# Attention stage of an attention and two-MoE kernel: another order of first loads, first products, weight splits and last slot sums

## The chip, the cores and the metric

The kernel runs on one core of a Trainium2 chip. The metric is the device time of one execution in microseconds (us); smaller is better. The engines are TensorE (PE), VectorE (DVE), ScalarE (ACT), GpSimd (POOL) and SyncE (SP); SP, ACT and POOL also issue the transfers (DMA).

## The reference

Attention with a decaying state, then two mixtures of experts (MoE), each sending a token to one of eight experts:

```python
for t in range(S):                       # 2 batches, 8 heads, S = 768, D = 64
    state = gamma * state + einsum('bhd,bhe->bhde', k[:, :, t], v[:, :, t])
    y[:, :, t] = scale * einsum('bhd,bhde->bhe', q[:, :, t], state)
x = y as 1536 tokens of 512
# first MoE: only tokens with x @ w_skip > 0; expert = argmax of x @ w_gate, gate = its softmax
out = x;  out[those] = x + gate * (relu(x @ w1[e]) @ w2[e])
# second MoE: all tokens, up to `capacity` for each expert; the others give 0
out = gate * (relu(x @ w1[e]) @ w2[e])
```

## The kernel before

**Tiling.** The 768 positions are six chunks `c` of 128, and each chunk has two units `(c, b)`, one for each batch. `load_chunk` brings a chunk into one tile `ain`: q and k with the heads first (for the scores), then, in a second load, k and v with the tokens first (parts 2 and 3). Chunk 0's q and k come as two loads, one for each batch. The constants come as three loads: on ACT's queue those with the mask and the decay factors for v, and `gq`, the decay for the outputs; on SP's queue, later, the rest.

**Work of a unit.** `scores` (line 515) are products of k and q on PE, two PSUM tiles, masked by DVE into `p` (line 524). `setup_v` scales v by the decay, on DVE for chunk 0 (line 507) and on ACT for the others (line 502). `state` (line 539) adds k v to a sum that stays in PSUM, and ACT copies it to `sbd` (line 545). `outs` multiplies q by that state (line 554) and `p` by v (line 564) into one PSUM tile, and DVE scales it by `g2[c]` into `xt` (line 572). The `g2` of chunks 1 to 5 are made by POOL at the very start (`setup_g`, line 492).

**Routing.** When both units of a chunk are done, `sink` (in `route_tokens`) multiplies `xt` by the gate weights and an identity in one product for each batch (line 254; here called the gate product; its operand `idw` is made by POOL, line 124). ACT copies the result to the rows `rowc` (line 258), DVE sums the logits `lg` (line 384), picks the expert (`m`, line 289), ACT writes the rows to a table in DRAM (line 322), PE ranks the tokens within each expert (lines 299 to 302), DVE turns ranks into one-hot rows `hot` (line 354) and adds the chunk's counts to `cum` (line 418), and PE sums row numbers by slot (line 439, the slot sums), which DVE adds to `idacc` (line 444). After chunk 4, expert 0's rows so far are gathered by these numbers into `a0` (line 329, POOL). In chunk 5 (`last`) the tokens for expert 0 aren't gathered: `place` (line 339) adds `a0` and the placed rows of chunk 5 in PSUM in two halves, which `half` splits into `xh` and `xl` (lines 359, 360), the first expert's operand. The numbers of all slots, `ida`, are cast behind that (line 313), and the other experts' tokens are gathered by them.

**Weights.** Each float32 operand of an expert product is split into a high and a low part, and three products are summed (lines 656 to 658). A weight chunk of 128 x 2048 is loaded by SP (line 174, three buffers), its high part is copied by ACT and the low part is subtracted by DVE. Four chunks are split during attention in quarters of 512 columns (`prep_quarters`, lines 203 and 215); the others during the experts (lines 223 and 231).

**Order.** The schedule is manual: instructions go to each engine in the order in which the program issues them. `main` is a generator; after each of its steps one step of the oldest `sink` in `side` and one of `pieces` (the quarter splits) is issued, so `idle(n)` puts work n steps later. A chunk has nine such steps. `warm` issues products of a zero tile that nobody reads.

Of the kernel before, what the change touches and what calls it, by code (L numbers as in the profile page):

```python
# [44 lines left out]
def kernel(  # L45
# [27 lines left out]
    def load_chunk(c, a_p, nbuf):  # L73
        t = a_p.tile([128, 4, B, 512], F32, tag="ain", name="ain", bufs=nbuf)
        if c:
            nc.sync.dma_start(out=t[:, 0:2], in_=qkv[c, :, 0:2])
        else:
            for b in range(B):
                nc.sync.dma_start(out=t[:, 0:2, b, :], in_=qkv[c, :, 0:2, b, :])
        nc.sync.dma_start(out=t[:, 2:4], in_=qkv[c, :, 2:4])  # L80
        return t

    cs = const.tile([128, C_N], F32, name="cs")
    first = load_chunk(0, a_p, 3)
    nc.scalar.dma_start(out=cs[:, C_MASK:C_ID], in_=cst[:, C_MASK:C_ID])
    nc.scalar.dma_start(out=cs[:, 0:C_MASK], in_=cst[:, 0:C_MASK])
# [110 lines left out]
    def prep_quarters(n):  # L197

        late = []
        for i in range(n):  # L200
            hi, lo, r3 = next_parts()
            for k in range(4):
                nc.scalar.activation(out=hi[:, k], in_=r3[:, k], func=ACTF.Copy)
                late.append((hi, lo, r3, k))
                if len(late) > 2:
                    lower(*late.pop(0))
                yield
            if i == 1:
                yield from idle(6)
        while late:  # L210
            lower(*late.pop(0))
            yield
# [154 lines left out]
    def route_tokens(rows, rows_p):  # L367
        def sink(c, xt, psum):
# [48 lines left out]
            for a in range(2):  # L417
                nc.vector.tensor_tensor(
                    out=cum, in0=cum, in1=m2d[:, 16 * a:16 * a + 16].unsqueeze(1).to_broadcast([128, 2, 16]), op=ALU.add
                )  # L420
            if not last:
                yield from idle(1 if c == NCH - 2 else 3)
# [19 lines left out]
            if last:  # L442
                half(1)
# [3 lines left out]
            if last:  # L447
                ids.append(numbers(idacc[:, 0, :], "ida"))
            yield
# [8 lines left out]
    def attention(a_p, ps, first, nbuf, sink, pump, g_tiles):  # L458
# [27 lines left out]
        def setup_g():  # L486

            g2.append(gq)
            for c in range(1, NCH):
# [90 lines left out]
        def main():  # L580
            setup_g()
            yield from scores(0, 0)
            yield from setup_v(0)
            for c, b in units:
                if b == 0:
# [5 lines left out]
                    if pump:  # L591
                        while nxt[0] < (0, 0, 2, NRAW)[min(c, 3)]:
                            load_w()
                        if c == 3:
                            pieces.append(prep_quarters(4))
                    yield from scores(c, 1)
                    yield from state(c)
                    yield from outs(c, 0)
# [515 lines left out]
```

## Time and profile before

| | |
|---|---|
| timed runs | median 400.8 us of 3 (399.2 to 401.15) |
| profiled execution | 402.8 us, of which the span of the trace is 401.0 |
| busy share of the span | PE 95%, weight loads 82%, DVE 65%, ACT 54%, POOL 17% |
| mean granted PE clock | 0.979 of full speed |
| instructions | 6615 |

How to read it: the profile is one execution, its times run from the first instruction, and a row of the timeline gives an engine's start, length, line and operands, and in brackets how long the engine was idle before and what ended that. A granted clock of 1.00 is 2.4 GHz, 0.50 is 1.2 GHz. Attention with its routing ends at about 86 us; the first MoE runs to about 210 and the second to the end.

### The profile page before, as it was taken

The page shows a single profiled execution, that of the slowest core. Times are in us where ns is not written, and L with a number is a line of the kernel's source. Part 1 is how long each engine was busy: PE and PEld are TensorE (multiplying, and loading weights), DVE is VectorE, ACT ScalarE, POOL GpSimd, SP SyncE. Part 2 cuts the span into 40 slices and gives each one's busy share as a digit, 9 for nine tenths or more (in the row PEclk, how much of TensorE's full clock was granted, in tenths as well). Part 3 has the DMA queues.
Part 4 walks back from the last instruction along what each step waited for, and adds up shares of the span by engine and source line. Part 5 has one row for each costly group of instructions (what it writes and reads, how often), then busy time and mean ns, then how long its engine had stood idle before and what let it go on. Part 6 is the DMA issues. An engine that isn't in the chain of part 4 may idle for free.

```text
span 401.0 us, 6615 instructions
## 1 busy us (share of the span) xinstructions
PE 381.3 (95%) x2610; PEld 326.9 (82%) x2611; DVE 262.2 (65%) x493; ACT 216.9 (54%) x283; POOL 68.5 (17%) x85
## 2 busy tenths in 40 slices
PE   6899998988999999999999999999999999999992
PEld 3788886776888788878778798998989899898982
DVE  2666789467899999999973577375483727546110
ACT  1455676157877778778641864464455446542201
POOL 5500000127010110000045120402203040211101
PEclk9899999599999999999999999999999999999998
DMA  8979954669999998898886395848576683320101
GB/s 305 403 276 391 417 198 161 211 236 395 377 322 371 347 325 305 334 339 318 294 282 195 131 328 202 286 147 276 196 253 198 205 279 136 129 83 0 52 2 40
DMA packets 17993, 97.69 MB, mean 244 GB/s; under 512 B 2975, under 2 KB 3103, under 8 KB 8356
## 3 DMA queue, kind: packets, MB, share of 16 engines
q1 hardware_dynamic: 12036, 80.03, 55.7%
q0 software_dynamic: 4000, 13.25, 9.5%
q10 hardware_dynamic: 1920, 3.93, 2.7%
q8 instruction: 22, 0.36, 0.4%
q14 instruction: 15, 0.12, 0.1%
HBM read 88.11 MB, written 10.14 MB: 245 GB/s over the span
## 4 chain that ended last, share of the span: by engine, by line
PE 76%; DVE 7%; issue 7%; DMA 6%; ACT 1%; POOL 0%; SPq 0%; POOLq 0%; ACTq 0%
PE s L656 10%; PE s L658 10%; PE s L657 10%; PE o L656 10%; PE o L658 10%; PE o L657 9%; DMA table<-rowc 3%; PE s L254 3%; PE t L649 2%; DMA ain<-in_qkv_dram 2%; PE m L564 2%; DVE lo L215 2%; PE t L239 2%; DMA xs<-table,ida 2%; PE t L867 1%
## 5 line engine op out<-in xcount | busy, mean ns | idle before, releaser
L231 DVE TENSOR_TENSOR lo<-raw,hi 128x2048 fp32r<-128x2048 f32 x60 | 136.3, 2284 | 5.6 <-ACT hi L223 5.6
L223 ACT ACTIVATE hi<-raw 128x2048 fp32r<-128x2048 f32 x60 | 114.8, 1914 | 17.5 <-PE o L658 15.7
L656 PE MATMUL o<-hi,hTh 128*128 128x512 f32 x192 | 78.1, 407 | 0.2 <-ACT hTh L359 0.2
L658 PE MATMUL o<-hi,hTl 128*128 128x512 f32 x192 | 75.5, 393 | 0.1
L657 PE MATMUL o<-lo,hTh 128*128 128x512 f32 x192 | 74.9, 390 | 0.0
L657 PE MATMUL s<-xl,hi 128*128 128x256 f32 x224 | 63.2, 282 | 0.0
L658 PE MATMUL s<-xh,lo 128*128 128x256 f32 x224 | 63.1, 282 | 0.0
L656 PE MATMUL s<-xh,hi 128*128 128x256 f32 x224 | 63.1, 282 | 0.0
L887 DVE SCALAR_TENSOR_TENSOR hTl<-s,hTh 128x512 fp32r<-128x512 f32 x28 | 19.4, 692 | 63.9 <-ACT hTh L886 63.9
L305 POOL DMA_INDIRECT out_dram<-y,ixo x16 | 20.1, 1255 | 143.8 <-ACT y L742 130.7
L658 PEld LDWEIGHTS o<-hi,hTl 128*128 128x128 f32 x192 | 36.0, 188 | 8.8 <-DVE hTl L360 0.7
L657 PEld LDWEIGHTS s<-xl,hi 128*128 128x128 f32 x224 | 42.7, 191 | 0.3
L656 PEld LDWEIGHTS s<-xh,hi 128*128 128x128 f32 x224 | 42.7, 191 | 0.3
L658 PEld LDWEIGHTS s<-xh,lo 128*128 128x128 f32 x224 | 42.6, 190 | 0.0
L656 PEld LDWEIGHTS o<-hi,hTh 128*128 128x128 f32 x192 | 36.1, 188 | 6.7 <-ACT hTh L359 0.5
L657 PEld LDWEIGHTS o<-lo,hTh 128*128 128x128 f32 x192 | 36.2, 188 | 6.6
L886 ACT ACTIVATE hTh<-s 128x512 fp32r<-128x512 f32 x28 | 16.7, 597 | 40.8 <-PE s L658 40.5
L656 PE MATMUL s<-hi,xh 128*128 128x512 f32 x80 | 33.3, 416 | 1.4 <-DVE idacc L444 1.1
L658 PE MATMUL s<-hi,xl 128*128 128x512 f32 x80 | 31.5, 394 | 0.0
L657 PE MATMUL s<-lo,xh 128*128 128x512 f32 x80 | 31.3, 392 | 0.0
L742 ACT ACTIVATE y<-o,xs 128x512 f32<-128x512 f32 x15 | 10.3, 689 | 33.0 <-PE o L658 27.2
L360 DVE TENSOR_TENSOR xl<-t,xh 128x512 fp32r<-128x512 f32 x23 | 15.2, 686 | 12.1 <-ACT xh L359 12.1
(147 smaller groups left out, 519.4 us busy)
## 6 DMA issues: line engine op xcount, KB each, us to landing
raw<-in_w1a_dram SPq DMA_DIRECT2D x16, 1024.0 KB, 7.0
raw<-in_w2a_dram SPq DMA_DIRECT2D x16, 1024.0 KB, 6.0
raw<-in_w1b_dram SPq DMA_DIRECT2D x16, 1024.0 KB, 4.9
raw<-in_w2b_dram SPq DMA_DIRECT2D x16, 1024.0 KB, 5.0
ain<-in_qkv_dram SPq DMA_DIRECT2D x11, 1024.0 KB, 8.7
table<-rowc ACTq DMA_DIRECT2D x6, 580.0 KB, 4.5
table<-row POOLq DMA_DIRECT2D x8, 290.0 KB, 6.6
ain<-in_qkv_dram SPq DMA_DIRECT2D x2, 512.0 KB, 4.5
```

The costliest lines, as they stand in the source:

```text
L215: nc.vector.tensor_tensor(out=lo[:, k], in0=r3[:, k], in1=hi[:, k].bitcast(F32), op=ALU.subtract)
L223: nc.scalar.activation(out=hi, in_=r3, func=ACTF.Copy)
L231: nc.vector.tensor_tensor(out=lo, in0=r3, in1=hi.bitcast(F32), op=ALU.subtract)
L254: nc.tensor.matmul(out=t[:, 128 * i:128 * i + KW], lhsT=xt(2 * g + i), rhs=idw[:, g, 17 - 17 * i:17 - 17 * i + KW], start=i == 0, stop=i = ...
L305: return nc.gpsimd.indirect_dma_start(out=dst[:, :], out_offset=bass.IndirectOffsetOnAxis(ap=idx, axis=0), in_=src, in_offset=None, bounds ...
L360: nc.vector.tensor_tensor(out=lo, in0=src, in1=hi.bitcast(F32), op=ALU.subtract)
L656: nc.tensor.matmul(out=acc, lhsT=a[0], rhs=w[0], start=first, stop=False)
L657: nc.tensor.matmul(out=acc, lhsT=a[0], rhs=w[1], start=False, stop=False)
L658: nc.tensor.matmul(out=acc, lhsT=a[1], rhs=w[0], start=False, stop=last)
L742: nc.scalar.activation(out=y, in_=acc, func=ACTF.Copy, scale=xs[:, GCOL + 1:GCOL + 2])
L886: nc.scalar.activation(out=hi[:, g:g + 2, :], in_=acc, func=ACTF.Relu)
L887: nc.vector.scalar_tensor_tensor(out=lo[:, g:g + 2, :], in0=acc, scalar=0.0, in1=hi[:, g:g + 2, :].bitcast(F32), op0=ALU.max, op1=ALU.subtract
```

## The change

- Chunk 0's load of parts 2 and 3 becomes two loads, v first, then k; of the constants on ACT's queue `gq` comes first.
- In chunk 0 the outputs of unit (0,0) are issued before the state, behind five `warm` products.
- `setup_g` makes the factors of chunks 1 to 4 at the start, that of chunk 5 in chunk 2.
- Weight loads begin a chunk earlier, the quarter splits begin in chunk 2 (two steps into it) instead of chunk 3, and the pause between the second and third weight chunk is two steps instead of six.
- The two sums of `cum` run on POOL. The slot sums of chunk 4 come one step later.
- In chunk 5 `idacc` and `ida` come before the second half of the placing.

```diff
@@ -77,13 +77,14 @@
         else:
             for b in range(B):
                 nc.sync.dma_start(out=t[:, 0:2, b, :], in_=qkv[c, :, 0:2, b, :])
-        nc.sync.dma_start(out=t[:, 2:4], in_=qkv[c, :, 2:4])
+        for i in ((2, 4),) if c else ((3, 4), (2, 3)):
+            nc.sync.dma_start(out=t[:, i[0]:i[1]], in_=qkv[c, :, i[0]:i[1]])
         return t
 
     cs = const.tile([128, C_N], F32, name="cs")
     first = load_chunk(0, a_p, 3)
+    nc.scalar.dma_start(out=cs[:, 0:C_MASK], in_=cst[:, 0:C_MASK])
     nc.scalar.dma_start(out=cs[:, C_MASK:C_ID], in_=cst[:, C_MASK:C_ID])
-    nc.scalar.dma_start(out=cs[:, 0:C_MASK], in_=cst[:, 0:C_MASK])
     idw = const.tile([128, 2, 164], F32, name="idw")
     cap_i = const.tile([1, 2], I32, name="cap_i")
     zb = const.tile([128, 2 * RW], BF16, name="zb")
@@ -197,6 +198,7 @@
     def prep_quarters(n):
 
         late = []
+        yield from idle(2)
         for i in range(n):
             hi, lo, r3 = next_parts()
             for k in range(4):
@@ -206,7 +208,7 @@
                     lower(*late.pop(0))
                 yield
             if i == 1:
-                yield from idle(6)
+                yield from idle(2)
         while late:
             lower(*late.pop(0))
             yield
@@ -415,11 +417,11 @@
             for b in range(B):
                 slot_hot(hot[:, b, :], sl[:, b:b + 1])
             for a in range(2):
-                nc.vector.tensor_tensor(
+                nc.gpsimd.tensor_tensor(
                     out=cum, in0=cum, in1=m2d[:, 16 * a:16 * a + 16].unsqueeze(1).to_broadcast([128, 2, 16]), op=ALU.add
                 )
             if not last:
-                yield from idle(1 if c == NCH - 2 else 3)
+                yield from idle(2 if c == NCH - 2 else 3)
             new = rk[:, 64:96]
             if last:
                 hi = x_p.tile([128, KT, 128], F32R, tag="xh", name="xh")
@@ -439,13 +441,12 @@
                     nc.tensor.matmul(
                         out=new[:, 16 * h:16 * h + 16], lhsT=hot[:, b, 128 * h:128 * h + 128], rhs=mrow[:, b, :], start=b == 0, stop=b == B - 1
                     )
-            if last:
-                half(1)
             nc.vector.tensor_tensor(out=idacc, in0=idacc, in1=new[:, 0:32].rearrange("p (h j) -> p h j", h=2), op=ALU.add)
             if c == NCH - 2:
                 gather(numbers(idacc[:, 0, 0:1], "id0"), t=a0)
             if last:
                 ids.append(numbers(idacc[:, 0, :], "ida"))
+                half(1)
             yield
         return sink
 
@@ -483,10 +484,9 @@
             step(side)
             step(pieces)
 
-        def setup_g():
-
-            g2.append(gq)
-            for c in range(1, NCH):
+        def setup_g(c0, c1):
+
+            for c in range(c0, c1):
                 pool, tag = g_tiles[c - 1]
                 t = pool.tile([128, 4, 128], F32, tag=tag, name="g2")
                 nc.gpsimd.tensor_tensor(
@@ -578,7 +578,8 @@
                 side.append(last.pop() if last else sink(c, xt[c], psum))
 
         def main():
-            setup_g()
+            g2.append(gq)
+            setup_g(1, NCH - 1)
             yield from scores(0, 0)
             yield from setup_v(0)
             for c, b in units:
@@ -589,13 +590,21 @@
                             constants()
                             no_rows()
                     if pump:
-                        while nxt[0] < (0, 0, 2, NRAW)[min(c, 3)]:
+                        while nxt[0] < (0, 2, NRAW)[min(c, 2)]:
                             load_w()
-                        if c == 3:
+                        if c == 2:
                             pieces.append(prep_quarters(4))
                     yield from scores(c, 1)
-                    yield from state(c)
-                    yield from outs(c, 0)
+                    if c:
+                        if c == 2:
+                            setup_g(NCH - 1, NCH)
+                        yield from state(c)
+                        yield from outs(c, 0)
+                    else:
+                        if pump:
+                            warm(psum(), 5)
+                        yield from outs(c, 0)
+                        yield from state(c)
                 else:
                     if c + 1 < NCH:
                         scale = setup_v(c + 1)
```

How it moves the instructions, in excerpts of the order in which engines get them.

PE at the start, behind the scores of both units of chunk 0, before (in the change from the last of the five added pairs on).

```order
L515 MATMUL s<-ain 128x128 x16
L539 MATMUL u<-ain 64x64 x16
L564 MATMUL m<-p,ain 64x128 x8
L515 MATMUL s<-ain 128x128 x8
L564 MATMUL m<-p,ain 64x128 x8
L515 MATMUL s<-ain 128x128 x4
L254 MATMUL s<-idw,xt 128x145 x4
```

In the change:

```order
L456 LDWEIGHTS zb
L456 MATMUL m<-zb 128x512
L564 MATMUL m<-p,ain 64x128 x8
L539 MATMUL u<-ain 64x64 x16
L515 MATMUL s<-ain 128x128 x8
L564 MATMUL m<-p,ain 64x128 x8
L515 MATMUL s<-ain 128x128 x4
L256 MATMUL s<-idw,xt 128x145 x4
```

The state (`u`) went behind the outputs of unit (0,0); the scores of chunk 1 and the gate product (line 254, now 256) follow as before.

PE in chunk 5, from the products of q and the state for its second unit to the second gate product; the slot sums of chunk 4 are line 439, now 441. Before:

```order
L554 MATMUL m<-ain,sbd 128x128 x4
L439 MATMUL s<-mrow,hot 128x16 x4
L254 MATMUL s<-idw,xt 128x145 x4
L564 MATMUL m<-p,ain 64x128 x8
L254 MATMUL s<-idw,xt 128x145 x4
```

In the change:

```order
L554 MATMUL m<-ain,sbd 128x128 x4
L256 MATMUL s<-idw,xt 128x145 x4
L564 MATMUL m<-p,ain 64x128 x8
L441 MATMUL s<-mrow,hot 128x16 x4
L256 MATMUL s<-idw,xt 128x145 x4
```

The slot sums moved behind the first gate product and the second unit's outputs.

DVE at the same place, from `mrow` of chunk 4 to the cast for the gather of `a0` (before).

```order
L392 TENSOR_TENSOR mrow<-m,cs 128x32
L215 TENSOR_TENSOR lo<-raw,hi 128x512 x2
L572 TENSOR_TENSOR xt<-m,g_141 128x4x128
L407 TENSOR_TENSOR pr<-s,m 128x32
L409 TENSOR_REDUCE sl<-pr 128x2
L354 TENSOR_SCALAR hot<-iota,sl 128x256 x2
L418 TENSOR_TENSOR cum<-cum,m 128x32 x2
L215 TENSOR_TENSOR lo<-raw,hi 128x512
L444 TENSOR_TENSOR idacc<-idacc,s 128x32
L313 CAST id_979<-idacc 128x1
```

In the change:

```order
L394 TENSOR_TENSOR mrow<-m,cs 128x32
L572 TENSOR_TENSOR xt<-m,g_473 128x4x128
L409 TENSOR_TENSOR pr<-s,m 128x32
L411 TENSOR_REDUCE sl<-pr 128x2
L356 TENSOR_SCALAR hot<-iota,sl 128x256 x2
L572 TENSOR_TENSOR xt<-m,g_473 128x2x128 x2
L444 TENSOR_TENSOR idacc<-idacc,s 128x32
L315 CAST id_1010<-idacc 128x1
```

The low-part subtractions of the weights (`lo`) are gone from here, and so is `cum`; the two `xt` halves of the second unit now come ahead of `idacc`.

## Rows read from the trace of the kernel before

**Rows 1.** Timeline of the start: start, length, engine, line, operation [idle before <-releaser].

```profile
6.41 5.48 POOL L492 TENSOR_TENSOR g<-cs 128x512 f32<-128x512 f32 x5 [3.60 <-DMA cs<-in_cst_dram]
...
7.32 1.29 DVE L524 TENSOR_TENSOR p<-s,cs 128x512 f32<-128x512 f32 x2 [5.71 <-PE s L515]
...
9.78 2.66 DVE L507 TENSOR_TENSOR ain<-ain,cs 128x512 f32<-128x512 f32 x2 [1.17 <-DMA ain<-in_qkv_dram]
...
11.05 0.69 PE L539 MATMUL u<-ain 128*64 128x64 f32 x16 [2.58 <-DVE ain L507]
...
15.77 0.53 POOL L124 COPY idw<-cs 128x128 f32<-128x128 f32 x2 [3.73 <-DMA cs<-in_cst_dram]
...
18.19 1.25 PE L254 MATMUL s<-idw,xt 128*128 128x145 f32 x8
```

**Rows 2.** Timeline, PE: second gate product of chunks 1 to 4.

```profile
30.59 1.25 PE L254 MATMUL s<-idw,xt 128*128 128x145 f32 x8
...
41.16 1.25 PE L254 MATMUL s<-idw,xt 128*128 128x145 f32 x8
...
53.24 1.25 PE L254 MATMUL s<-idw,xt 128*128 128x145 f32 x8 [0.49 <-DVE xt L572]
...
63.81 1.25 PE L254 MATMUL s<-idw,xt 128*128 128x145 f32 x8
```

**Rows 3.** Stretches: length; PE, PEld, DVE, ACT, POOL busy; PE clock; DMA share, GB/s.

```profile
20.00:30.00 10.00, 10.00 (x131) 8.87 (x129) 6.87 (x25) 5.05 (x14) 0.19 (x1) 1.00 0.74 278
...
70.00:72.00 2.00, 1.78 (x7) 1.78 (x8) 1.92 (x8) 0.00 (x0) 0.00 (x0) 0.57 1.09 311
```

**Rows 4.** Timeline from 70 us: last chunk, and the first expert products.

```profile
70.22 1.07 PE L439 MATMUL s<-mrow,hot 128*128 128x16 f32 x4 [1.87 <-DVE hot L354]
...
71.56 0.15 DVE L313 CAST id<-idacc 128x1 int32<-128x1 f32 x1
...
72.43 1.25 POOL L329 DMA_INDIRECT a<-table,id  x1 [19.31 <-DVE lo L215]
...
75.96 2.27 PE L254 MATMUL s<-idw,xt 128*128 128x145 f32 x8 [0.62 <-DVE xt L572]
...
78.88 2.27 PE L455 MATMUL s<-zb 128*128 128x512 bf16 x6 [0.22 <-issue]
...
79.86 0.19 DVE L289 TENSOR_TENSOR m<-t,tm 128x32 bf16<-128x32 f32 x1
...
81.06 1.14 PE L339 MATMUL m<-cs,a 128*128 128x128 f32 x8
...
86.20 0.47 PE L656 MATMUL s<-hi,xh 128*128 128x512 f32 x1 [1.12 <-DVE idacc L444]
...
87.21 1.04 POOL L329 DMA_INDIRECT xs<-table,ida  x1 [13.32 <-DVE idb L791]
...
93.48 0.66 PE L649 MATMUL t<-cs,xs 128*128 128x128 f32 x4 [1.12 <-DMA xs<-table,ida]
```

**Rows 5.** Chain that ended last, start and duration, PE in chunk 0 to 1.

```profile
20.09 1.18 PE s L254 x8
...
22.36 1.09 PE m L554 x8
...
23.45 1.02 PE m L564 x16
...
26.82 0.35 PE s L439 x4
```

**Rows 6.** Instructions by line: the split copies on ACT, the subtractions on DVE.

```profile
L203 ACT ACTIVATE hi<-raw x16: 612/616/632, 40.9 to 69.2; 128x512 fp32r<-128x512 f32 x16
...
L215 DVE TENSOR_TENSOR lo<-raw,hi x16: 681/685/693, 44.8 to 76.1; 128x512 fp32r<-128x512 f32 x16
```

**Rows 7.** DMA issues from 70 to 74 us: gather of `a0`, microseconds to landing.

```profile
a<-table,id POOLq DMA_INDIRECT x1, 3.7
```

**Rows 8.** Weight loads of line 174 up to 100 us, time to landing.

```profile
DMA to landing us min/median/max: 4.8/8.1/12.2
```

## The prediction

> **What bounds the kernel now.** I read the busy shares first: TensorE (PE) is busy 95% of the span, so a gain must come from a stretch in which PE waits or runs at the lower of its two clock levels. The chain that ended last shows PE nearly without a break from 95 us on; that part should keep its length and only start earlier. All that the diff touches lies before, in the attention stage, up to about 86 us. There I read the timeline.
>
> At the start, DVE finishes the masked scores of unit (0,0) at 7.32 + 1.29 = 8.61 and then waits for v; its two products with v start at 9.78, and PE, idle for 2.58 us, starts again at 11.05 [rows 1]. The first gate and router products (line 254) run at 18.19, although their operand idw is complete at 15.77 + 0.53 = 16.30 [rows 1].
>
> In the middle, the second such product of each chunk tells the pace: 30.59, 41.16, 53.24, 63.81 [rows 2]. 10.57 us is a chunk in which PE is the bound; the one from 41.16 to 53.24 took 12.08, 1.51 more, and it is the first with weight splits on DVE.
>
> In the last chunk, PE waits 1.87 us for `hot`, and then works at the low level: 0.57 granted from 70 to 72 [rows 3], and the product of line 254 takes 2.27 [rows 4] where it takes 1.18 at the high level [rows 5]; the warm-up products from 78.88 are still slow, 0.38 us each [rows 4].
>
> **The change, part by part.** The sum is against the profiled execution's 402.8 us; the median of the timed runs is 400.8, and I carry the difference over to that.
>
> *A, the start.* v comes in a load of its own, ahead of k. Of the 1 MB that ended at 9.78 it is the first half, so it is there about when DVE is free at 8.61. v's first product then ends at 8.61 + 1.33 = 9.94 (half of the 2.66 in [rows 1]), 1.1 earlier than PE's start at 11.05. The five added warm-ups lie in PE's wait from 8.5 on. Before, PE needed 18.19 - 11.05 = 7.14 from there to the first gate products, with a wait for v's second half and partly at the low level; the new order (outputs ahead of the state) has the second half ready when it is wanted. The same 7.14 from 9.94 gives 17.1, a gain of 1.1; without the wait PE is earlier than idw, and 16.3 to 16.4 is the floor, a gain of 1.8. I take **-1.8**, ends -1.1 and -1.9: what is ahead of the gate products then fits before the floor. The order of the two constant loads on ACT I cost at nothing: the mask is wanted by 7.32, and both loads together had ended when POOL's multiplies, which read both, started at 6.41 [rows 1]. The multiply for chunk 5 moved to chunk 2 costs POOL 1.1 us where POOL has nothing else. SP issues one load more, 0.5 us; its queue holds a backlog of loads until 15, so nothing lands later for it.
>
> *B, splits from chunk 2 on.* Each of the 16 quarter splits takes ACT 0.616 and DVE 0.685 [rows 6]. Before, 6, 5 and 5 of them lay between the logit sums of chunks 2, 3, 4 and 5; now 6, 7, 3 and 0 lie between those of chunks 1 to 5. DVE was busy 6.87 of 10 us in a free stretch [rows 3], so 7.26 of 10.57, which leaves 3.3. Six splits want 4.1 and seven want 4.8: 0.8 and 1.5 too much. Three stand as one block ahead of `xt` and `hot` of chunk 4; the two sums of `cum`, now POOL's, give a little back. I put the excess at 2.5 where before had 1.5: **+1.0**. If DVE's overhang is absorbed, it is -1.5; if the block of three (2.05) is paid in full too, 4.3 - 1.5 = +2.8. On POOL the `cum` sums wait for `m` and the ranks, and behind them now stands the copy of the next chunk's token numbers, which ran ahead before; the row write on ACT wants it a chunk later, 10 us of cover. ACT holds: 5.05 of 10 [rows 3] is 5.34 a chunk, and eight splits add 4.93, under 10.57.
>
> Here a row and a rule can be weighed. DVE's two products with v took 1.33 each while POOL's five multiplies ran beside them until 11.89 [rows 1]; a split of the same 512 columns takes 0.685 with POOL idle [rows 6]. The second product was no shorter though POOL ended 0.55 before it, so the row does not settle whether POOL was the cause. The Trainium skill, GPSIMD Engine Reference, Key points, says that GpSimd shares its SBUF interfaces with VectorE and contends with DVE instructions that have two SBUF inputs, which the splits are; by that rule the `cum` sums on POOL slow them, and if each of the four in the two full chunks held DVE up by 0.2, an estimate (the small product for `m` lasts 0.19, [rows 4]), the sum would be 0.8 worse. I leave that out of the sum.
>
> *C, the last chunk.* No split is left there, and the slot sums of chunk 4 (line 439), for which PE waited, come two products later. Counting at the high level from the start of chunk 4's second gate product (63.81 before): 1.18 for it, 1.09 and 1.02 for the outputs, 0.2 for the ranks, 1.09, 1.18, 1.02, 0.35 and 1.18 [rows 5], with 0.3 of waits for `xt`, make 8.6 to the end of the last gate product; `m` follows 1.8 later (79.86 + 0.19 against 75.96 + 2.27, [rows 4]), ranks at 10.6, where before had 81.06 - 63.81 = 17.25. So PE could be 6.6 earlier. But something else is late next: the product with `a0` needs the gather, which needs the moved slot sums. These ended at 71.29 before, the cast ran at 71.56, the gather was issued at 72.43 [rows 4] and landed 3.7 later [rows 7], 4.84 after them. Now they end at 7.1 + 0.2, so `a0` is there at about 12.2, and PE waits 1.6. From there to 86.20 nothing changes: 17.25 - 12.2 gives **-5.0**.
>
> *D, the gather of the tokens.* The tokens of the next expert were gathered from 87.21 on, after sums that stood behind the second `xl`, and PE waited 1.12 for them at 93.48 [rows 4]. With the sums ahead of the second half of placing, DVE does them about 1.25 earlier, after the first `xl`. **-1.0**; 0 if the gather waits for the last rows' write instead, -1.1 at most.
>
> *E, the clock in the new wait.* No row shows what a wait of 1.6 costs: 1.87 was followed by the low level [rows 3, 4], two of 1.12 (at 86.20 and 93.48, [rows 4]) were not. Below it is nothing. Above it is all the work from `a0` to 86.20, 5.14 less 1.12 idle, at half pace: +4.0. The wait is nearer to the one that fell, but follows eight dense products; I take half of that work, **+2.0**.
>
> Sum: -1.8 + 1.0 - 5.0 - 1.0 + 2.0 = **-4.8**, so 398.0 for a profiled execution and **396.0** against the median.
>
> **The rivals.**
> 1. *The clock holds* through the wait for `a0`: E is 0, **394.0**. For it, 1.6 is shorter than 1.87; against it, only 0.3.
> 2. *The clock falls and stays down* until the expert products: E is +4.0, **398.0**. For it, the low stretch of before outlasted its cause by some 10 us.
> 3. *The low stretch is not in the timed runs.* Then most of C was never there. At the high level before would run 0.35, 1.18, 1.02, 0.4 of wait, 1.18 and 1.8 from 70.22, 76.15 instead of 81.06: 4.9 less. The gain is then -1.8 + 1.0 - 0.1 - 1.0 = -1.9, **399.0**: the change doesn't do what it seems to. Against it: such a run would take 402.8 - 4.9 = 397.9, and the lowest of three is 399.2.
> 4. *Weights come too late, slower.* The third weight chunk is loaded at chunk 2's start behind 2 MB of chunk 4, and its first split stands in ACT's order ahead of v's scaling and the row copies. It is wanted 13 steps later, at nine a chunk 15.3 us; the longest weight load of before took 12.2 [rows 8]. From 15.3 on each microsecond is paid by every engine; at 22 the gain is gone and 2 more, with 23 it is **404**.
>
> **How the numbers follow.** About 0.5% (2.0 us) is what a measurement can tell from no change. The forecast has 0.32, rival 1 0.28, rival 2 0.18, rival 3 0.16, rival 4 0.06. Faster by over 0.5% (under 398.8) are the first three, **0.78**; within it rival 3, **0.16**; slower **0.06**. The range must reach rivals 1 to 3: below, 394.0 less about 1 for B's better end, 392.9; above, rival 3 with 0.8 for B's worse half, **399.8**. B at its worst ends and rival 4 are left out.
>
> **What would show it.** Right: the first gate product near 16.4; second gate products with one long chunk, and the last at some 61 to 63 for chunk 4; no wait at the slot sums of chunk 4; the last gate product at 1.2 to 1.3; a wait before the product with `a0`; the first expert product near 80; PE no longer waiting at the first gathered tokens. Wrong: gate products still near 18 (A); two long chunks or DVE late into chunk 5 (B); a first expert product after 84 (C, E); or the gain gone again by 110.

## The result, and the profile after

| | before | after |
|---|---|---|
| timed runs beside each other | median 401.36 us, 11 runs (398.32 to 403.12) | median 396.63 us, 11 runs (396.16 to 399.02) |
| ratio after / before | | 0.9897, 95% interval 0.9867 to 0.9928 |
| profiled execution (span) | 402.8 (401.0) | 396.63 (394.9) |
| mean granted PE clock, profiled execution | 0.979 | 0.996 |

By this ratio the change is faster by 1.0% (0.7 to 1.3%); 396.0 was forecast. In the profiled executions the gain is larger, 6.2 us, since that of before lies 1.4 above its median and that of after at its own.

**The start**, timeline of the kernel after on PE, DVE and POOL (columns as in [rows 1]). Lines have moved: the gate product of line 254 is line 256, the POOL copy of line 124 is line 125.

```profile
8.43 1.25 PE L456 MATMUL m<-zb 128*128 128x512 bf16 x5
10.48 1.09 PE L564 MATMUL m<-p,ain 128*64 128x128 f32 x16 [0.79 <-DVE ain L507]
15.95 1.25 PE L256 MATMUL s<-idw,xt 128*128 128x145 f32 x8 [0.69 <-POOL idw L125]
...
8.84 1.58 DVE L507 TENSOR_TENSOR ain<-ain,cs 128x512 f32<-128x512 f32 x1
10.35 0.68 DVE L507 TENSOR_TENSOR ain<-ain,cs 128x512 f32<-128x512 f32 x1
...
15.61 0.29 POOL L125 COPY idw<-cs 128x128 f32<-128x128 f32 x1 [5.58 <-DMA cs<-in_cst_dram]
```

The first gate product runs at 15.95 where it ran at 18.19 [rows 1], and PE now waits 0.69 for `idw`: the floor of step A is reached. Two stretches of before, then the same two of after (columns as in [rows 3]), show that the low clock at the start is gone too, 0.56 and 0.58 against 1.00:

```profile
12.00:14.00 2.00, 1.50 (x22) 1.51 (x24) 1.64 (x3) 0.27 (x1) 0.04 (x1) 0.56 0.97 400
14.00:16.00 2.00, 2.00 (x24) 1.67 (x22) 0.63 (x1) 1.98 (x6) 0.23 (x1) 0.58 1.13 374
```

```profile
12.00:14.00 2.00, 2.00 (x42) 1.81 (x40) 1.20 (x3) 1.19 (x2) 0.00 (x0) 1.00 0.98 403
14.00:16.00 2.00, 1.31 (x21) 0.95 (x17) 1.51 (x3) 1.31 (x5) 0.39 (x2) 1.00 1.13 372
```

**The middle**, timeline of after, PE: the second gate product of chunks 1 to 4 (against [rows 2]), with the waits between them; then ACT around the second of the two waits.

```profile
28.56 1.25 PE L256 MATMUL s<-idw,xt 128*128 128x145 f32 x8
...
39.13 0.76 PE L256 MATMUL s<-idw,xt 128*128 128x145 f32 x4
40.55 0.76 PE L256 MATMUL s<-idw,xt 128*128 128x145 f32 x4 [0.65 <-ACT rowc L260]
...
50.62 0.76 PE L256 MATMUL s<-idw,xt 128*128 128x145 f32 x4
51.71 0.76 PE L256 MATMUL s<-idw,xt 128*128 128x145 f32 x4 [0.33 <-ACT rowc L260]
...
58.33 0.76 PE L441 MATMUL s<-mrow,hot 128*128 128x16 f32 x4 [0.31 <-DVE hot L356]
...
62.52 0.76 PE L256 MATMUL s<-idw,xt 128*128 128x145 f32 x4
```

```profile
50.09 1.14 ACT L205 ACTIVATE hi<-raw 128x512 fp32r<-128x512 f32 x2
51.26 0.69 ACT L260 ACTIVATE rowc<-s 128x273 f32<-128x273 f32 x2
51.83 0.63 ACT L205 ACTIVATE hi<-raw 128x512 fp32r<-128x512 f32 x1
52.35 0.69 ACT L260 ACTIVATE rowc<-s 128x273 f32<-128x273 f32 x2
```

The chunks take 10.57, 11.49 and 11.90 us; no single one takes 12.08 as before, but two are long. The gate product of a chunk now waits in its middle for ACT, whose two copies of gate rows stand between split copies. The stretch from 15.95 to 62.52 is 46.57 us long where before had 45.62 (18.19 to 63.81): the middle costs 0.95.

**The last chunk**, timeline of after (against [rows 4]): PE, then DVE, POOL and SP's loads.

```profile
69.19 0.61 PE L441 MATMUL s<-mrow,hot 128*128 128x16 f32 x4
...
74.52 1.16 PE L341 MATMUL m<-cs,a 128*128 128x128 f32 x8 [1.28 <-DMA a<-table,id]
...
79.49 0.50 PE L665 MATMUL s<-hi,xh 128*128 128x512 f32 x1 [0.94 <-DVE xl L362]
...
87.32 0.66 PE L658 MATMUL t<-cs,xs 128*128 128x128 f32 x4 [1.65 <-DMA xs<-table,ida]
```

```profile
70.19 0.15 DVE L315 CAST id<-idacc 128x1 int32<-128x1 f32 x1
...
78.22 0.17 DVE L315 CAST ida<-idacc 128x16 int32<-128x16 f32 x1
...
70.64 1.25 POOL L331 DMA_INDIRECT a<-table,id  x1 [3.91 <-DVE id L315]
...
79.34 1.03 POOL L331 DMA_INDIRECT xs<-table,ida  x1 [5.46 <-ACT xh L361]
...
78.70 0.33 SPq L175 DMA_DIRECT2D raw<-in_w1a_dram  x1
79.08 4.44 SPq L175 DMA_DIRECT2D raw<-in_w2a_dram  x2
```

The slot sums no longer wait, the 1.28 before `a0` is the new wait, and the first expert product comes 6.71 earlier than before. At the gathered tokens PE waits 1.65 where it waited 1.12: 0.5 is given back there. PE's clock is at the high level in every slice of the page but the last, as in the kernel before.

### The profile page after: what moved, and what is told of

Read it like the earlier page. It is cut to its first block, busy times and chain, and to the rows that moved or that the text cites. A ratio compares the mean times of both kernels' runs of the same rounds, so it can differ in the third digit from the quotient of the medians.

```text
span 394.9 us, 6637 instructions
## 1 busy us (share of the span) xinstructions
PE 377.5 (96%) x2616; PEld 322.9 (82%) x2616; DVE 260.6 (66%) x481; ACT 216.4 (55%) x283; POOL 69.8 (18%) x97
## 4 chain that ended last, share of the span: by engine, by line
PE 77%; DMA 7%; issue 6%; ACT 5%; DVE 3%; POOL 1%; ACTq 0%; POOLq 0%; DVEq 0%
PE o L665 11%; PE s L665 10%; PE o L667 10%; PE s L667 10%; PE s L666 10%; PE o L666 10%; DMA cs<-in_cst_dram 4%; PE t L658 3%; PE s L256 2%; ACT hi L205 2%; DMA xs<-table,ida 2%; PE t L241 2%; PE t L876 1%; PE m L564 1%; ACT ain L502 1%
## 5 line engine op out<-in xcount | busy, mean ns | idle before, releaser
L524 DVE TENSOR_TENSOR p<-s,cs 128x512 f32<-128x512 f32 x24 | 15.4, 683 | 12.7 <-PE s L515 12.7
```

The costliest lines, as they stand in the source:

```text
L524: nc.vector.tensor_tensor(out=t, in0=sa[j].rearrange("p (r t) -> p r t", r=4), in1=mask.unsqueeze(1).to_broadcast([128, 4, 128]), op=ALU.mult,
```

## The experiments

The runs came in three groups on three chips: u1 to u4; n1 to n3 and c1; w0, g1 and the two f. Each group was timed beside the kernel before on its own chip, whose medians there were 401.3, 402.2 and 401.5. So times of different groups can differ by up to some 0.9 us for the chip alone; the ratios allow for that. The table also splits the runs by their mean granted clock: within one kernel the runs below 0.994 are nearly always the longer ones.

| run | median us (range, runs) | ratio to before, 95% interval | runs at 0.994 or more / below |
|---|---|---|---|
| after | 396.63 (396.16 to 399.02, 11) | 0.9897 [0.9867, 0.9928] | 7 / 4 |
| u1_start | 398.75 (396.6 to 400.36, 9) | 0.9929 [0.9901, 0.9957] | 4 / 5 |
| u2_splits | 402.13 (400.77 to 403.55, 12) | 1.0017 [0.9995, 1.0039] | 0 / 12 |
| u3_slots | 397.13 (396.59 to 398.08, 6) | 0.9904 [0.9881, 0.9928] | 4 / 2 |
| u4_ida | 396.39 (395.94 to 397.17, 6) | 0.9881 [0.9858, 0.9904] | 6 / 0 |
| n1_late_loads | 399.57 (398.88 to 400.74, 6) | 0.9938 [0.9914, 0.9963] | 3 / 3 |
| n2_fill | 395.88 (395.54 to 400.23, 6) | 0.9868 [0.9829, 0.9908] | 4 / 2 |
| n3_both | 398.52 (397.91 to 401.7, 8) | 0.9927 [0.9897, 0.9957] | 6 / 2 |
| c1_cum | 396.07 (395.9 to 396.28, 5) | 0.9849 [0.9825, 0.9873] | 5 / 0 |
| w0_nowarm | 398.21 (396.69 to 398.98, 10) | 0.9914 [0.9894, 0.9933] | 4 / 6 |
| g1_early | 396.02 (395.9 to 396.3, 6) | 0.985 [0.9805, 0.9894] | 6 / 0 |
| f1_best | 395.25 (395.11 to 396.71, 6) | 0.9837 [0.9792, 0.9883] | 5 / 1 |
| f2_second | 395.16 (394.98 to 395.32, 6) | 0.9828 [0.9783, 0.9872] | 6 / 0 |

The kernel before, timed in the same three groups, had no run above 0.991 (48 runs).

**The start undone** (u1_start): one load for parts 2 and 3, mask first, state ahead of the outputs, no warm-ups.

```diff
-        for i in ((2, 4),) if c else ((3, 4), (2, 3)):
+        for i in ((2, 4),):
...
-                        if pump:
-                            warm(psum(), 5)
-                        yield from outs(c, 0)
                         yield from state(c)
+                        yield from outs(c, 0)
```

> The changed kernel with its start undone: v and k in one load again, the mask ahead of gq, the state ahead of the outputs of unit (0,0), no five warm-ups. If the start is worth what the traces show, the first gate product is back at about 18.2 us instead of 15.95 and the first expert product some 2.2 later, so 398.5 to 399 timed. Rival: the pace from there on is set by the splits on DVE and ACT, which absorb an earlier start; then the first expert product moves by under 1 us and the time is under 397.8.

The first gate product came at 17.37, not at 18.2 as expected, and the low clock from 12 to 16 us was back (0.50 and 0.69); the last second gate product came at 63.90, 1.38 after that of the change, so nothing of it was absorbed in the middle. Undoing this part costs 2.1 us by the medians and 1.3 by the ratios; its runs at the high clock lie only some 0.8 above those of the change (medians 397.3 and 396.45), which suggests that part of its worth is in the clock. Its profiled execution (399.99 us) also shows what the wait for `a0` can do; PE, then a stretch with the granted clock as the third number from the end:

```profile
76.14 1.60 PE L341 MATMUL m<-cs,a 128*128 128x128 f32 x8 [1.52 <-DMA a<-table,id]
...
78.81 1.68 PE L341 MATMUL m<-oh,rowc 128*128 128x128 f32 x8
```

```profile
75.00:80.00 5.00, 3.86 (x17) 3.16 (x18) 1.61 (x8) 0.00 (x0) 0.24 (x1) 0.67 0.36 141
```

After a wait of 1.52 the clock fell: 1.60 and 1.68 where the change has 1.16 and 1.05, and 0.67 granted from 75 to 80. The length of the wait does not decide it: in w0_nowarm, below, PE waited longer for `a0` and the clock stayed at the high level.

**The split schedule undone** (u2_splits): the weight loads, the start of the quarter splits and the pause as before.

```diff
-        yield from idle(2)
...
-                yield from idle(2)
+                yield from idle(6)
...
-                        while nxt[0] < (0, 2, NRAW)[min(c, 2)]:
+                        while nxt[0] < (0, 0, 2, NRAW)[min(c, 3)]:
...
-                        if c == 2:
+                        if c == 3:
```

> The changed kernel with the split schedule undone: weight loads and quarter splits start a chunk later, with the pause of six steps; the slot sums of chunk 4 stay moved. Theory splits: what helped the last chunk is that no split stands ahead of hot on DVE; now they do again, the last gate product comes 2 to 4 us later against chunk 4's second gate product than in the changed kernel, partly by a low clock, and the time is 398.5 to 400.5, though the middle gets up to 1 us back. Rival slot sums: moving them behind the outputs hides the wait whatever stands on DVE; then PE waits under 0.5 us there, the clock holds, and the time is 396 to 397.5.

402.13: without the earlier splits the rest of the change gains nothing. Where the time goes, in PE's, POOL's and SP's timelines and in the issue of the gather of `a0` (last number: microseconds to landing):

```profile
67.14 1.25 PE L255 MATMUL s<-idw,xt 128*128 128x145 f32 x8 [1.28 <-DVE xt L571]
...
77.32 1.42 PE L340 MATMUL m<-cs,a 128*128 128x128 f32 x8 [3.87 <-DMA a<-table,id]
...
70.79 1.43 POOL L330 DMA_INDIRECT a<-table,id  x1 [4.26 <-DVE id L314]
...
71.12 12.34 SPq L175 DMA_DIRECT2D raw<-in_w1a_dram  x2
...
a<-table,id POOLq DMA_INDIRECT x1, 6.5
```

The gather goes out 0.15 us later than in the change, but takes 6.5 us instead of the 3.7 of [rows 7] and the 3.8 of the change. The late splits free a weight buffer at 71, and SP sends the next 1 MB load 0.33 behind the gather. PE waits 3.87 and its clock is 0.81 from 75 to 80. With the late splits of before, the same kind of load went out at 68.33 and then at 76.77, either side of the gather.

From the second gate product of chunk 4 (61.42) to the first expert product (83.94) it takes 22.52 us, the change 16.97. Of these 5.55, only 1.34 lie ahead of the end of the gate products, where 2 to 4 were expected: the wait of 1.28 for `xt`, behind the splits on DVE. The rest is 2.6 more of wait for `a0` and 1.65 of low clock behind it. So the splits cost PE less through DVE's order than through the load that they hold back until the gather, and the time missed the expected 398.5 to 400.5.

**The slot sums of chunk 4 put back** (u3_slots): `idle(1)` for `idle(2)`.

> The changed kernel with the slot sums of chunk 4 back ahead of the first gate product of chunk 5. Theory a0: with the splits gone hot is ready about 1.0 us after PE gets there, which costs PE that wait, but the sums end some 1.5 us earlier, so the gather of a0 lands before PE wants it and its wait of 1.28 disappears; the product with a0 starts within 0.5 us of 74.5, and the time is 396 to 397.5. Rival slot sums: the move itself is what saves; undone, the first expert product comes over 1 us later and the time is 398 or more.

PE waits 0.73 for `hot` and 0.53 for `xt`, and then not at all for `a0`:

```profile
67.45 0.76 PE L441 MATMUL s<-mrow,hot 128*128 128x16 f32 x4 [0.73 <-DVE hot L356]
...
70.85 1.25 PE L256 MATMUL s<-idw,xt 128*128 128x145 f32 x8 [0.53 <-DVE xt L572]
```

1.26 of wait takes the place of 1.28. Its runs at the high clock are at 396.59 to 397.15, those of the change at 396.16 to 397.61: this edit alone, with the splits gone, is worth nothing that can be measured. With the late splits it is worth nothing either: u2_splits, which keeps the move, takes 22.52 from chunk 4's second gate product to the first expert product, the kernel before 22.39 (63.81 to 86.20).

**`ida` after the second half again** (u4_ida): `half(1)` ahead of the sums of `idacc`, as before.

> The changed kernel with the sums for ida behind the second half of the placing again. Step D of the prediction: the gather of the tokens is issued about 1.2 us later against the first expert product, and PE waits that much longer for it, 2.8 instead of 1.65, so 397.5 to 398. Rival loads: the gather lands when the weight loads issued just before it are through (about 8.5 us after the first of them in both traces), so a later issue costs nothing: PE's wait stays at 1.4 to 1.9 and the time within 0.4 of the changed kernel.

No loss: 396.39. The gather, its microseconds to landing, and PE:

```profile
80.39 1.03 POOL L331 DMA_INDIRECT xs<-table,ida  x1 [6.63 <-DVE idb L801]
...
xs<-table,ida POOLq DMA_INDIRECT x1, 6.7
...
87.16 0.66 PE L659 MATMUL t<-cs,xs 128*128 128x128 f32 x4 [1.54 <-DMA xs<-table,ida]
```

It was issued 1.05 later than in the change, landed 6.7 later, and PE waited 1.54 for it: the rival with the loads holds.

**The weight loads behind the gather** (n1_late_loads).

```diff
-    for _ in range(NRAW2):
-        load_w()
     nc.vector.tensor_copy(out=idb, in_=idacc[:, 1, 8:16])
     prep_hi()
     prep()
+    for _ in range(NRAW2):
+        load_w()
```

The counter that says which loads use the two added buffers starts at 3 instead of -1, as the loads' order asks.

> The two 1 MB weight loads that go out at 78.70 and 79.08, just ahead of the gather of the next expert's tokens (79.34), are issued after the first whole-chunk preparation instead, behind the gathers. Theory 1, the gather lands late because those loads are ahead of it (it lands about 8.5 us after them in the kernel before, in the change and in the run with the splits undone, whenever it was issued): it then lands some 4 us after its issue, near 83.5, PE's wait of 1.65 at 87.32 is gone, and the kernel is 1.3 to 1.6 us faster than the change, about 395.1. Theory 2, the gather takes 6 to 8 us whatever else moves: wait 1.65 as before, time the same or up to 2 us worse because the weights come later. Theory 3: the wait is gone, but the later weights cost it again further on: time within 0.5 of the change, with a new wait between 90 and 130 us.

The first half of theory 1 holds: the gather of the tokens lands in 3.5 us, and PE's wait for it is gone. The kernel is slower all the same: by 2.7 us in the lowest runs (398.88 against 396.16), by 1.6 in the ratios, whose intervals just overlap. The gather's issue, ACT's longest waits from 86 to 104 us, and PE:

```profile
xs<-table,ida POOLq DMA_INDIRECT x1, 3.5
```

```profile
ACT hi L225 <- DMA raw<-in_w2a_dram: 5.3, 2, 3.1
ACT hi L225 <- DMA raw<-in_w1a_dram: 2.5, 2, 1.3
```

```profile
103.94 0.66 PE L715 MATMUL t<-cs,row 128*128 128x128 f32 x4 [1.64 <-DVE row L701]
...
107.33 1.06 PE L241 MATMUL t<-idw,x2t 128*128 128x8 f32 x8 [1.34 <-ACT x2t L717]
```

The weights, loaded 4 us later, are late for ACT by 7.8 us in four waits, and DVE and ACT, each working in order, bring `row` and `x2t` late behind them. That is theory 3, with a price larger than the gain. In this profile the clock fell too, to 0.73 from 110 to 115, behind these waits.

**Six warm-up products into the wait for `a0`** (n2_fill), in place of the three behind it.

```diff
                 acc = [psum("m"), psum("m")]
+                warm(pt(), 6)
                 place(acc, a0, ident, True, False)
-                warm(pt(), 3)
```

> Six warm-up products stand ahead of the product with a0 instead of three behind it: they lie in PE's wait of 1.28 us, at 73.2 to 74.6, so PE works there. Theory 1, the timed runs differ because PE's clock falls in some of them after that wait: the runs of the change (396.2 to 399.0) draw together near 395.9 to 396.4, median about 395.8, and the first expert product comes at 78.9 instead of 79.49, since the three products behind are gone. Theory 2, the runs differ for another reason (the start, the waits in the middle): the spread of 2 to 3 us stays, and only the 0.6 is gained, or lost again in the wait for the gathered tokens.

The wait is filled, and the first expert product comes at 78.80. The runs at the high clock are at 395.54 to 396.03, 0.6 below those of the change in the lowest and 0.7 in the medians, as expected of the three products. But two of six runs fell to 397.1 and 400.23, at 0.991 and 0.988: the wait for `a0` is not the only cause of the spread.

**Both of these** (n3_both):

> Both of these edits at once. If both theories 1 hold: 1.65 of wait and 0.6 of warm-ups gone, some 394.2 to 394.8 and a spread under 1 us. If the gather is late whatever moves, the 0.6 goes into its wait: 396.4. If later weights cost it again: 395.5 to 396.5 with a new wait beyond 90 us.

398.52; the waits for `row` and `x2t` were 1.82 and 1.50, and one of 0.77 came behind them. Late weights decide again. On the same chip n2_fill, which differs in the loads alone, has 395.88: 2.6 us for the late loads, and its runs at the high clock all lie below all of these.

**`cum` back on DVE** (c1_cum): `nc.vector` for `nc.gpsimd` in the two sums. **POOL's multiply for chunk 5 earlier** (g1_early): `setup_g(NCH - 1, NCH)` at `c == 1` instead of `c == 2`, `cum` on POOL.

> The two running sums of `cum` per chunk are back on DVE, all else is the change. Theory 1, DVE and ACT are both behind the splits in chunks 2 and 3 and DVE's 0.38 us per chunk is hidden, since ACT's row copies are what PE waits for: second gate product of chunk 4 at 62.5 as now, time the same within 0.4 us (396.6). Theory 2, they are on the path in the two full chunks: +0.4 to +0.8 us, and longer waits for `hot`. Theory 3, the sums on POOL slow DVE's splits: this kernel is faster, by up to 0.8 us.

> POOL's multiply for chunk 5 is issued one chunk earlier, ahead of the first running sums of `cum` instead of behind them; the sums stay on POOL. In the change it ran at 23.12 beside `hot`, and the two `hot` of that chunk took 1.19 us together; with `cum` on DVE it ran at 18.58 and they took 0.62. Theory 1, the sums on POOL cost only through this: they make the multiply wait, and its port use slows `hot`. Then `hot` takes 0.62 here too, the distance from the first gate product of chunk 0 to the second of chunk 1 is 12.40 instead of 12.61, and the kernel is 0.2 faster than the change, as the kernel with `cum` on DVE. Theory 2, the sums themselves slow DVE or the row copies: distance 12.61 still, time as the change.

Both are at 396.0 to 396.1, with all their runs at the high clock. The second chunk's `hot` and POOL's multiply, first in the change, then in g1_early:

```profile
23.39 1.19 DVE L356 TENSOR_SCALAR hot<-iota,sl 128x256 fp32r<-128x256 f32 x2
...
23.12 1.04 POOL L492 TENSOR_TENSOR g<-cs 128x512 f32<-128x512 f32 x1
```

```profile
23.33 0.62 DVE L356 TENSOR_SCALAR hot<-iota,sl 128x256 fp32r<-128x256 f32 x2
...
18.60 1.03 POOL L492 TENSOR_TENSOR g<-cs 128x512 f32<-128x512 f32 x1
```

From the first gate product of chunk 0 to the second of chunk 1 both take 12.40 us, the change 12.61: 0.21 for the multiply that stood behind the `cum` sums, which wait for PE's ranks. It ran 4.5 us late, beside `hot`. From there to chunk 4's second gate product c1_cum takes 33.90 and the change 33.96, so there the sums themselves cost nothing on either engine. c1_cum's third theory is wrong as it was put (the splits were not slowed), and right in its sign.

**The five warm-ups at the start left out** (w0_nowarm).

> The five warm-up products in PE's wait at the start (8.4 to 9.6 us) are left out, all else is the change. Theory 1, they keep PE's clock up, which is 1.00 from 12 to 16 us with them and was 0.56 to 0.58 there before: the stretch from 10 to 15 us is granted about 0.7, PE loses some 1.2 us, of which the wait of 0.69 for idw takes a part, first gate product at 16.4 to 16.6 instead of 15.7 to 16.0, time +0.4 to +0.7. Theory 2, the earlier products with v alone keep it up: first gate product at 15.7 to 16.0 and the time within 0.3 of the change. In a few runs the low clock may stay longer, which would show as runs of 398 to 400.

Its profiled execution answers theory 2: clock 1.00 from 8 to 18 us, first gate product at 15.83. It also has the longest wait for `a0` after which the clock held; PE, then a stretch:

```profile
74.80 1.16 PE L341 MATMUL m<-cs,a 128*128 128x128 f32 x8 [1.72 <-DMA a<-table,id]
```

```profile
75.00:80.00 5.00, 4.07 (x32) 3.60 (x32) 1.42 (x6) 1.51 (x3) 0.39 (x1) 1.00 0.26 78
```

Its runs at the high clock, 396.69 to 397.02, are some 0.5 above those of the change (medians 396.96 and 396.45), but six of ten are at 397.94 to 398.98. Four of eleven of the change are at 397.65 or more, so these numbers do not tell whether the warm-ups keep runs from falling.

**`cum` on DVE and the filled wait together** (f1_best): c1_cum and n2_fill in one.

> The two edits that gained, together: `cum` on DVE, and six warm-up products ahead of the product with a0 in place of three behind it. If they add: undisturbed runs at 395.2 to 395.5 (395.6 with the fill alone, 396.0 with `cum` alone), first expert product at about 78.2; the wait for the gathered tokens (1.7 to 1.8) stays. If the gather and the weight loads set the end of this stretch, the second gain disappears in that wait: 395.7 to 396.

395.25, ratio 0.9837 [0.9792, 0.9883], with the first expert product at 78.28: the two gains add. The interval overlaps that of the change; the five runs at the high clock (395.11 to 395.41) all lie below every run of the change, and below every run of g1_early on the same chip (395.9 to 396.3).

**The second load later** (f2_second): f1_best, with one of the two loads sent from ACT.

```diff
-    for _ in range(NRAW2):
-        load_w()
+    load_w()
...
     prep_hi()
+    load_w(nc.scalar)
     prep()
```

> As the one before, and the second of the two 1 MB weight loads ahead of the gather goes out from ACT's queue after the first whole-chunk copy, at about 80.8 instead of 79.1; the first stays. Theory 1, the gather's delay grows with the bytes ahead of it, and 1.7 us is not enough to make the weights late: the wait of 1.7 falls to 0 to 0.6 and the time by 0.7 to 1.5 us, to 394.0 to 394.7. Theory 2, DMA is the bound from 79 to 110 us, and whatever the gather gains the weights lose, as when both loads were put back by 4 us: no gain or up to 1.5 us slower, with waits of ACT for `raw` and of PE for `row` or `x2t` near 104. Theory 3, one load is enough to hold the gather: wait as before, time the same.

This tested nothing: the load went out at 77.58, ahead of the first whole-chunk copy and of the gather (78.23), not at 80.8.

```profile
77.58 0.35 ACTq L175 DMA_DIRECT2D raw<-in_w2a_dram  x1
```

The gather took 7.7 us and PE's wait was 1.5; the time is that of f1_best.

## Why the prediction was right, and where its steps were not

The forecast of 396.0 was 0.6 too low, and its sum of -4.8 agrees with the -4.7 of the medians. That closeness is partly luck. Against the profiled execution, for which the sum was made, the gain is 6.2: D was 1.5 too good, E took 2.0 that was not paid, and A and C gave 0.9 more than forecast. Before's profile is 1.4 above its median, so the medians lie closer together than the profiles. The 2.0 that E took off the gain made up for this, though the median run of the change (0.996) did not pay it either. The steps:

- **A, -1.8 forecast, -2.24 measured.** The floor was named rightly (`idw`, PE waits 0.69), and the place of PE's earlier start too. It was mis-sized twice. DVE came to v's first product at 8.84, not 8.61, and took 1.58 for it, not 1.33 (before, the two took 1.21 and 1.52), so PE started at 10.48 and not at 9.94; the wait for `idw` hid that. The floor itself lies at 15.95 instead of 16.3: the first gate product started behind the first of the two copies of `idw` (15.61 + 0.29), where the prediction counted both. Undone alone, this part gave back 1.42 in the profile: the rest of the 2.24 probably comes with POOL's shorter list of multiplies, which u1_start kept. There the second product with v took 0.68, where it took 1.52 before; no run tested the list by itself.
- **B, +1.0 forecast, +0.95 measured.** The size was right, the step to it was not, and the prediction's own sign of a wrong B, two long chunks, came. Of the 0.95, 0.21 is POOL's multiply in chunk 1 and 0.74 the two chunks with splits. DVE's overhang was to pay; but the waits are for ACT's row copies, 0.65 and 0.33, behind the split copies in ACT's order, with 0.31 for `hot` behind the block of three. The sentence "ACT holds" was right of the sum (10.27 of 10.57 us) and wrong of the order: split copies stood ahead of the row copies that PE waited for. The step "The multiply for chunk 5 moved to chunk 2 costs POOL 1.1 us where POOL has nothing else" failed: it stood behind `cum`, ran beside `hot`, and cost 0.21.
- **C, -5.0 forecast, -5.42 measured.** The mechanism was right: the splits left the last chunk, the slot sums no longer wait, the gather of `a0` is late next, and PE waits 1.28 (1.6 forecast). u2_splits shows that the earlier splits carry it, and u3_slots that the slot sums' move, which the text gave a share, carries none of it. That the gain comes by the wait for `hot` and the low clock behind it is read from the trace of before: in u2_splits, where the sums were moved, the late splits cost by another way, a load beside the gather. What had not been seen is how thin the cover of the gather is: one weight load behind it makes it 2.7 us longer.
- **D, -1.0 forecast, +0.5 measured.** This step failed, and not where it looked for its risk. "DVE does them about 1.25 earlier" came true: `ida` was cast at 78.22, 1.27 ahead of the first expert product, where before it stood 0.12 ahead of it. The gather went out 1.12 behind the cast, as before (1.13): against the first expert product it was issued 1.16 earlier. The last rows' write, the prediction's other end, did not hold it; issued at 73.57, it landed 3.8 later, ahead of the cast. What failed is that it would land as long after its issue as before. Before it landed 6.2 after its issue; in the change PE got the rows 7.98 after it. The cast and the landing of before:

```profile
86.08 0.17 DVE L313 CAST ida<-idacc 128x16 int32<-128x16 f32 x1
...
xs<-table,ida POOLq DMA_INDIRECT x1, 6.2
```

In the change the gather stood right behind two 1 MB loads (78.70 and 79.08), in u4_ida 1.9 behind the first. In both PE had the rows 8.6 to 8.7 after the first load, in the kernel before 8.3: the loads set the landing, and not the issue. With these loads put back the gather took 3.5 (n1_late_loads). u4_ida shows what the step is worth: nothing.

- **E, +2.0 forecast, 0 in the profiled execution.** There the clock held, as in rival 1, which said 394.0; D and the medians' smaller distance kept the time from it. Over the timed runs it is between: seven of eleven at 396.2 to 397.6, four at 397.65 to 399.0. The price was sized well: in u1_start, where it fell after that wait, PE took 4.11 us from the product with `a0` to the last slot sums (76.14 to 80.25), against 2.45 in the change (74.52 to 76.97): 1.7 more. But its condition, a wait near 1.87, does not decide: the clock fell after 1.52 in u1_start and held after 1.72 in w0_nowarm. That E was nothing in the profile and in the median run was, as far as these runs show, not to be read from the wait.

Of the rivals, 3 (the low stretch is not in the timed runs) does not hold as it was put: none of the 48 timed runs of before has more than 0.991, and most of those of the change have 0.994 or more. But they reach down to 0.978, the profile being among the low ones at 0.979, and the medians show 1.4 less gain than the profiles: part of the low stretches seems to be missing from many timed runs. No such run was profiled. Rival 4 named a real danger at the wrong place: no weight was late in the attention stage, but in n1_late_loads 4 us of delay in the first expert cost 1.6 to 2.9 net (ratios, medians).

What stays open is why the clock falls in some runs of the change and in none of c1_cum, g1_early, u4_ida and f2_second. Filling the wait for `a0` did not end it (2 of 6 in n2_fill), and leaving that wait open did not bring it (0 of 11 in c1_cum and g1_early). One difference goes with it: in the four kernels in which POOL's multiply no longer ran beside `hot` (c1_cum, g1_early, f1_best, f2_second) one run of 23 is below 0.994, in the change, u3_slots, u4_ida and n2_fill 8 of 29, in n1_late_loads, n3_both and w0_nowarm 11 of 24. That is a hint and was not tested; no falling run of the change was profiled.

## What to carry to other kernels

Work taken out of a stretch in which one wait brings on the next (late splits, a buffer freed late, a load beside a small gather, a wait, a low clock) can gain more than its own length (here 5.4 us, for a first wait of 1.87); look for such a stretch before counting instructions. A small gather on which PE waits should be followed through everything that releases it (its numbers, the rows that it reads, loads that run beside it) before its numbers are made earlier. And an engine whose busy time fits a stretch can still be late in it: read the order in which it does the work, not the sum.

## What the runs showed of the hardware

- Some DVE instructions took about twice as long beside POOL's multiplies of 512 columns. The product with v took 1.58 beside them and 0.68 after them, in one kernel; that settles what the prediction left open. The two `hot` took 1.19 against 0.62. The masked scores, which read PSUM, took 1.29 for two beside the same multiplies [rows 1]. The Trainium skill, GPSIMD Engine Reference, Key points, names DVE instructions with two SBUF inputs, or in a 2-port perf mode, as those that contend; the product with v is of the first kind, and agrees. `hot` has one tensor input and a column of scalars, and was slowed as well; no run shows in which mode it ran. The splits have two inputs and were not slowed by small work on POOL: beside the `cum` sums three of them took 1.94 in all, while the two sums took 1.16 instead of 0.57.
- A gather of some rows took 3.5 to 3.8 us where no 1 MB load was issued from 4 us ahead of it until it landed, and 6.2 to 8.1 with one or two such loads of another queue issued from 2.0 ahead of it to 0.3 behind it. The Trainium skill, DMA: Bandwidth & Descriptors, Queues, rings and completion order, says that each DMA engine takes turns between the queues that have work; the runs agree that a queue of its own does not protect a gather.
- Executions of one program on one chip differed by up to 4 us with the mean granted clock (u1_start: 396.6 at 0.996, 400.36 at 0.987); a single profile shows one of them.
